# Attention and feed-forward on one core: another issue order and engine choice for the same 2621 pieces of work

## The chip, the cores and the metric

The kernel runs on one core of one Trainium2 chip. The metric is the device time of one execution in microseconds (us); lower is better. A core has TensorE (PE, its weight loads PEld), VectorE (DVE), ScalarE (ACT), GpSimd (POOL) and SyncE (SP), which here only issues transfers. Each engine takes its instructions strictly in the program's order.

## The reference

Rotary attention over 4 batches of 8 heads (576 positions, head size 64), then a feed-forward block with SiLU. Cut to what is computed:

```
q_rot, k_rot = (rotate(q), rotate(k))
scores = scale * np.matmul(q_rot, k_rot.transpose(0, 1, 3, 2))
scores = scores - np.max(scores, axis=-1, keepdims=True)
attn = np.exp(scores)
attn = attn / (np.sum(attn, axis=-1, keepdims=True) + 1e-09)
x = np.matmul(attn, v)            # then heads beside each other: 2304 x 512
h = x @ w_in                      # 512 x 2048
g = h * (1.0 / (1.0 + np.exp(-h)))
out = g @ w_out                   # 2048 x 512
```

## The kernel before

Heads go in pairs (4 pairs `p` a batch `b`). A batch's rows are split into two **units** of 256 rows (`u` = 0 to 7, the odd one with 64 more rows that are gathered in `x_rem` and make a ninth unit, `rem`). A **slot** is 128 rows of scores of one head (or 64 rows of both heads of a pair): 144 slots in all. The feed-forward's hidden size is cut in 8 steps of 256, so there are 9 x 8 = 72 steps.

f32 values go through the f16 matmul as a high part and a remainder. On every path that means two passes over a tile: `hi` (`part_hi`, L322: one scaled copy to f16, on ACT, DVE or POOL) and `lo` (`part_lo`, L328: the remainder, on DVE or POOL). **The engine decides how many instructions `lo` is:** on DVE it is one with two tensor inputs (L330); on POOL it is two, a scaling in place (L318) and a subtraction (L333):

```
if e is dve:
    dve.scalar_tensor_tensor(out=lo, in0=src, scalar=s, in1=hi, op0=ALU.mult, op1=ALU.subtract)
else:
    times(e, src, src, s, 1.0)
    e.tensor_tensor(out=lo, in0=src, in1=hi, op=ALU.subtract)
```

A slot (`add_slot`, L845) goes: `S` scores on PE (L865 for batch 0, where q and k are f32, L873 and L879 else) into one of two PSUM buffers `s`; `max` on DVE; `neg`; `exp` on ACT (L905) into `e` (3 buffers); `nr0`, `nr1` (sum and reciprocal); `hi` and `lo` into `pn` (3 buffers); `T`, a transposing transfer on SP's queue (L931, L934) into `pt`. The maximum has two forms. Engine letter `d`: a plain reduction (L894) that `neg` follows on ACT (L900) or DVE. Letter `D`: the scores are scaled in place, and the running minimum comes out with them (L889 and an accumulator read); no `neg` follows.

`add_pv` (L947) multiplies a pair's 4 or 5 transposed slots by v on PE (L972) and makes `xh` and `xl`. `add_step` (L1009) is one feed-forward step: `m1` (L1027, 24 matmuls), `tanh` on ACT (L1037, L1039), `g` on DVE (L1043), `gh` and `gl` as `hi` and `lo` above, and two `m2` (L1083). `add_qk` rotates q and k of batches 1 to 3 (`rope`, three passes, L534, L538, L541, on DVE or POOL), takes `qhi` and `qlo`, and transposes by transfer. `add_qk_first` does batch 0 in f32: PE transposes (`qP`), `qE` copies out of PSUM. `add_w` packs and splits the weights on their way in (`wld`, `wT`, `wC`, `wX`, `wtr`, `whi`, `wlo`). PE's stream mixes steps of unit `u` with the slots of later units.

**What sets the order.** Each of these pieces is a part with a number. `ORDER` (L38) is one list of all 2621 numbers, each with the letter of an engine: `t` PE, `a` ACT, `d` or `D` DVE, `p` POOL, `s` SP's queue, `A` a transfer on ACT's queue. The last loop of the kernel runs the parts in that order, and each engine gets its own parts in it. A part that waits holds up all parts behind it on its engine. Buffers rotate in the order of first use.

Of the kernel before, what the change touches and what calls it, by code (L numbers as in the profile page):

```python
# [43 lines left out]
509d 536s 718a 731d 74p 732a 556s 719d 733a 721t 89d 722d 723d 724a 711s 90t 739t 87d 702s 734d 720s 40d 91d 41d 735d
97s 70p 557a 736a 95s 740d 741d 742a 743a 522t 521d 725d 42d 43p 737d 523d 86s 537a 524t 525d 726d 727p 738s 538a 748t
96s 526t 92d 44s 744d 745a 75d 527d 749D 528d 750d 728d 729s 746p 751a 752a 71t 775t 93d 72a 106d 99a 45d 529d 540s
753d 98a 76t 776d 777a 778a 112d 539d 747s 77a 784t 757t 754a 558a 785d 94d 786a 532p 755d 779a 113p 758D 759d 559d
530a 114p 533p 787a 1981t 1982a 766t 760a 1983d 761d 762d 584s 793t 100t 534a 531d 780d 101d 781d 102d 763a 764p 542a
# [20 lines left out]
985a 2123t 2120d 991t 127d 1004a 986d 992d 971p 987d 988p 2124a 2125d 1009t 668a 167d 1005d 972s 2126p 1010D 993a
1999t 994a 149s 2000d 151a 989d 990s 995a 671p 1006a 1011a 2001d 1007d 996d 997p 2121t 2122t 1018t 152t 1012a 1036t  # L70
669d 2130t 1008s 672a 2127p 2128t 153d 154d 1013a 1037d 998d 1038a 999s 1039a 2129t 1019d 1020a 1040a 155d 126d 1014d
1015p 677d 2131a 2132d 1021a 2133a 190s 673d 1016d 1022a 179s 1023d 156a 1027t 1028d 2134p 1029a 1024a 1030a 1041d
# [1123 lines left out]
```

## Time and profile before

| | us |
|---|---|
| time, median of 3 runs | 687.45 (685.22 to 689.85) |
| the profiled execution, its own time | 688.31 |
| its span, first to last instruction | 686.5 |

PE is busy for 90% of the span, DVE for 73%, POOL for 61%, ACT for 57%. PE's granted clock is 0.93 over the span. The profile gives each engine's busy time by stretch, groups of equal instructions with their mean duration, and who ended an engine's idle time. A busy engine can also be an engine that waits inside an instruction, so for the instructions of interest the shortest duration stands beside the mean.

### The profile page before, as it was taken

How to read it: one execution, taken by the hardware profiler on the slowest of the kernel's cores; microseconds unless marked ns; L12 is line 12 of the kernel's file. 1: busy time of each engine (PE TensorE's matmuls, PEld its weight loads, DVE VectorE, ACT ScalarE, POOL GpSimd, SP SyncE). 2: the span in 40 equal slices, each digit the busy share in tenths (PEclk: the TensorE clock that was granted, in tenths of full speed). 3: DMA queues.
4: the chain of work that ended last, by engine and by line, in shares of the span. 5: the costliest groups of instructions: out<-in, count | busy, mean ns of one | idle time of the engine just before them, and what ended most of it. 6: DMA issues, size and time to landing. Idle time of an engine off the chain costs nothing. (4 is left out here: it accounts for less than half of the span.)

```text
span 686.5 us, 12772 instructions
## 1 busy us (share of the span) xinstructions
PE 618.2 (90%) x4524; PEld 403.1 (59%) x4524; DVE 500.1 (73%) x1095; ACT 390.1 (57%) x828; POOL 419.9 (61%) x375
## 2 busy tenths in 40 slices
PE   2788779989998999998999899899999899999996
PEld 1555546655655566665656566565666666666663
DVE  4776878999899789897898898788787476421222
ACT  1556776787677686675656565655645555212221
POOL 0564688879875556775767848776695675222321
PEclk9755657999999999999999999999999999999999
DMA  6898847978886958889795786987775575510201
GB/s 183 237 240 194 208 112 186 237 182 195 150 163 120 191 93 180 141 149 146 154 206 89 144 159 139 174 154 157 131 128 87 76 121 96 84 32 1 48 1 31
DMA packets 227888, 94.73 MB, mean 138 GB/s; under 512 B 206704, under 2 KB 211568, under 8 KB 227824
## 3 DMA queue, kind: packets, MB, share of 16 engines
q1 hardware_dynamic: 227344, 93.03, 66.6%
q10 hardware_dynamic: 480, 0.89, 0.9%
q8 instruction: 35, 0.57, 0.3%
q14 instruction: 29, 0.24, 0.1%
HBM read 35.55 MB, written 4.72 MB: 59 GB/s over the span
## 5 line engine op out<-in xcount | busy, mean ns | idle before, releaser
L1027 PEld LDWEIGHTS <-w_in 128*128 128x128 f16 x1728 | 168.5, 99 | 41.7 <-issue 7.7
L1027 PE MATMUL m<-xh,w_in 128*128 128x256 f16 x1024 | 182.9, 277 | 4.2 <-DVE g L1043 3.7
L1083 PE MATMUL m<-w_out,gh 128*128 128x512 f16 x576 | 173.3, 383 | 0.6 <-DVE ob L318 0.6
L905 ACT ACTIVATE e<-s,small 128x576 f32<-128x576 f32 x144 | 111.9, 777 | 73.5 <-DVE small L318 19.0
L1027 PE MATMUL m<-xl,w_in 128*128 128x256 f16 x512 | 141.7, 277 | 3.3 <-DVE xl L990 3.3
L1083 PE MATMUL m<-w_out,gl 128*128 128x512 f16 x288 | 110.2, 383 | 2.4 <-POOL gl L333 2.1
L1043 DVE SCALAR_TENSOR_TENSOR g<-g,m 128x512 f32<-128x512 f32 x72 | 49.0, 681 | 71.0 <-ACT g L1039 39.3
L333 POOL TENSOR_TENSOR pn<-e,pn 128x576 f16<-128x576 f32 x68 | 96.6, 1420 | 5.7
L318 POOL TENSOR_SCALAR e<-e,small 128x576 f32<-128x576 f32 x68 | 65.9, 969 | 49.7 <-ACT pn L324 28.3
L894 DVE TENSOR_REDUCE small<-s 128x1 f32<-128x576 f32 x97 | 72.2, 748 | 21.3 <-PE s L865 15.8
L330 DVE SCALAR_TENSOR_TENSOR pn<-e,small,pn 128x576 f16<-128x576 f32 x76 | 78.0, 1029 | 13.1 <-ACT pn L324 7.2
L1083 PEld LDWEIGHTS <-gh 128*128 128x128 f16 x576 | 53.2, 100 | 54.4 <-issue 4.5
L318 POOL TENSOR_SCALAR pn<-e,small 128x576 f16<-128x576 f32 x52 | 46.7, 899 | 54.4 <-DMA pt<-pn 23.2
L873 PE MATMUL s<-Tk,Tq 128*128 128x512 f16 (+1 forms) x384 | 62.1, 287 | 12.0 <-ACT e L905 10.6
L324 ACT ACTIVATE pn<-e,small 128x576 f16<-128x576 f32 x71 | 54.7, 770 | 30.2 <-DMA pt<-pn 15.0
L1039 ACT ACTIVATE g<-m,small 128x512 f32<-128x512 f32 x64 | 43.6, 681 | 49.0 <-PE m L1027 37.0
L972 PE MATMUL pv<-pt,vh 128*64 128x256 f16 (+1 forms) x576 | 64.9, 297 | 1.4 <-DVE small L299 0.9
L318 POOL TENSOR_SCALAR g<-g,small 128x512 f32<-128x512 f32 x37 | 28.9, 780 | 58.4 <-ACT gh L324 41.8
L865 PE MATMUL s<-Tk,Tq 64*128 64x512 f32 (+3 forms) x160 | 57.8, 561 | 3.3 <-ACT e L905 3.0
L873 PEld LDWEIGHTS <-Tq 128*128 128x128 f16 x384 | 29.6, 99 | 40.1 <-issue 16.2
L1083 PEld LDWEIGHTS <-gl 128*128 128x128 f16 x288 | 28.4, 98 | 39.8 <-POOL gl L333 5.0
L333 POOL TENSOR_TENSOR gl<-g,gh 128x512 f16<-128x512 f32 x37 | 48.1, 1301 | 3.1
(166 smaller groups left out, 998.6 us busy)
## 6 DMA issues: line engine op xcount, KB each, us to landing
w_out<-in_moe_w_out_dram SPq DMA_DIRECT2D x4, 1024.0 KB, 5.5
w_in<-in_moe_w_in_dram SPq DMA_DIRECT2D x4, 1024.0 KB, 6.0
out_dram<-ob SPq DMA_DIRECT2D x28, 128.0 KB, 2.4
io<-in_q_dram SPq DMA_DIRECT2D x12, 288.0 KB, 3.5
io<-in_k_dram SPq DMA_DIRECT2D x12, 288.0 KB, 3.8
io<-in_v_dram SPq DMA_DIRECT2D x12, 288.0 KB, 4.0
io<-in_v_dram SPq DMA_DIRECT2D x13, 256.0 KB, 4.4
ring<-in_moe_w_in_dram SPq DMA_DIRECT2D x3, 1024.0 KB, 6.8
```

Of the source, the lines that this page charges most:

```text
L318: e.tensor_scalar(out=out, in0=in0, scalar1=s1, scalar2=s2, op0=ALU.mult, op1=ALU.bypass if s2 is None else ALU.mult)
L324: act.activation(hi, src, AF.Copy, scale=s)
L330: dve.scalar_tensor_tensor(out=lo, in0=src, scalar=s, in1=hi, op0=ALU.mult, op1=ALU.subtract)
L333: e.tensor_tensor(out=lo, in0=src, in1=hi, op=ALU.subtract)
L865: pe.matmul(o[:, c0:c1], tq[hs, qs], tk[hs, c0:c1], start=True, stop=True)
L873: pe.matmul(o, tq[:, j, 2 * c:2 * c + 2, :], kt[:, r0:r1, js], start=(n == 0), stop=(n == 1))
L894: dve.reduce_max(out=m_of(0, 1), in_=buf("s", i)[:, 0:S], axis=AX.X)
L905: act.activation(buf("e", i), buf("s", i)[:, 0:S], AF.Exp, bias=m_of(1, 2), scale=-1.0 if fused[i] else cc[0], accum_out=m_of(2, 3),)
L972: pe.matmul(o[64 * j:64 * j + 64, 0:m], vt[part][:, j, s, :], pt[:, a, j, 0:m], start=(z == 0), stop=(z == len(steps) - 1),)
L1027: pe.matmul(t[:, c, 0:n], w[:, wz, kk, fs], xx[:, kk, 0:n], start=(kk == 0 and x == 0), stop=(kk == KD - 1 and x == 2),)
L1043: dve.scalar_tensor_tensor(out=g, in0=g, scalar=1.0, in1=t, op0=ALU.add, op1=ALU.mult)
L1083: pe.matmul(o, gs[gz][:, c, ts], w[:, wz, c], start=(first and c == 0 and x == 0), stop=(last and c == 1 and x == 2),)
```

## The change

Only `ORDER` changes. The same 2621 parts stand in another order, with other letters for 549 of them (476 if the two forms of `max` count as one); no instruction's shape changes. The list's first line:

```
-494s 4s 496p 495a 497d 0d 1s 10d 3s 5d 2s 11d 12d 25s 13t 6d 14a 7d 8t 490s 9a 31d 26d 15s 32d 27d 500t 501d 685t 491a
+494s 3s 496d 495a 1s 4s 497d 2s 5d 10d 6d 11d 12d 13t 14a 25s 26d 7d 490s 31d 27d 8t 32d 57s 9d 685t 28p 491a 492a
```

PE's own sequence keeps its shape: parts change places with near neighbours. The engines' letters, counted over both lists (parts that changed sides cancel):

| part | before | after |
|---|---|---|
| `lo` (remainder of a slot) | DVE 76, POOL 68 | DVE 89, POOL 55 |
| `gl` (remainder of a step) | DVE 35, POOL 37 | DVE 49, POOL 23 |
| `qlo` | DVE 16, POOL 8 | DVE 21, POOL 3 |
| `hi` (high part of a slot) | ACT 71, DVE 21, POOL 52 | ACT 88, DVE 22, POOL 34 |
| `rope`, single passes | DVE 51, POOL 45 | DVE 58, POOL 38 |
| `max`, form `d` / form `D` | 97 / 47 | 58 / 86 |
| `neg` that is left | ACT 61, DVE 36 | ACT 35, DVE 23 |
| `nr0` | ACT 79, DVE 65 | ACT 87, DVE 57 |
| `qE` | ACT 8 | ACT 4, DVE 4 |
| `vhi` | ACT 11, DVE 1, POOL 4 | ACT 10, DVE 5, POOL 1 |

Three places in the order. First DVE, just ahead of the last `xl` of unit 1 (L990), for which the first step of that unit waits. The names are tiles with the number of the buffer: `rt` and `io` belong to `rope`, `vl` to v's remainder, `pn` and `e` to a slot. Before:

```order
L534 TENSOR_TENSOR rt_1998<-io_1965,sin_t_124 128x576
L330 SCALAR_TENSOR_TENSOR pn_1986<-e_1961,small_118,pn_1986 128x576
L330 SCALAR_TENSOR_TENSOR vl1_130<-io_1689,small_118,vh_1850 128x320
L894 TENSOR_REDUCE small_118<-s_1993 128x1
L990 SCALAR_TENSOR_TENSOR xl_1401<-pv_2003,small_118,xh_1400 128x256
L990 SCALAR_TENSOR_TENSOR x_rem1_122<-pv_2003,small_118,x_rem0_121 128x64
```

After:

```order
L894 TENSOR_REDUCE small_118<-s_1944 128x1
L919 RECIPROCAL small_118<-small_118 128x1
L534 TENSOR_TENSOR rt_2009<-io_1912,sin_t_124 128x576
L330 SCALAR_TENSOR_TENSOR vl1_130<-io_1754,small_118,vh_1904 128x320 x2
L990 SCALAR_TENSOR_TENSOR xl_1343<-pv_1961,small_118,xh_1342 128x256
L990 SCALAR_TENSOR_TENSOR x_rem1_122<-pv_1961,small_118,x_rem0_121 128x64
L330 SCALAR_TENSOR_TENSOR pn_1949<-e_1937,small_118,pn_1949 128x576
```

The slot's remainder (`pn`) moved from ahead of `xl` to behind it; a second piece of v's remainder moved ahead of it.

Second POOL, over the slots 70, 68 and 71 ahead of the score matmul of slot 76 in unit 4. Before:

```order
L318 TENSOR_SCALAR g_3448<-g_3448,small_118 128x512
L333 TENSOR_TENSOR gl_3471<-g_3448,gh_3464 128x512
L318 TENSOR_SCALAR pn_3487<-e_3400,small_118 128x576
L318 TENSOR_SCALAR e_3400<-e_3400,small_118 128x576
L333 TENSOR_TENSOR pn_3487<-e_3400,pn_3487 128x576
L318 TENSOR_SCALAR pn_3597<-e_3467,small_118 128x576
L318 TENSOR_SCALAR vh_3537<-io_3444,small_118 128x1152
L318 TENSOR_SCALAR e_3516<-e_3516,small_118 128x576
L333 TENSOR_TENSOR pn_3611<-e_3516,pn_3611 128x576
```

After:

```order
L318 TENSOR_SCALAR e_3280<-e_3280,small_118 128x576
L333 TENSOR_TENSOR pn_3370<-e_3280,pn_3370 128x576
L318 TENSOR_SCALAR pn_3483<-e_3427,small_118 128x576
L318 TENSOR_SCALAR e_3427<-e_3427,small_118 128x576
L333 TENSOR_TENSOR pn_3483<-e_3427,pn_3483 128x576
L318 TENSOR_SCALAR e_3509<-e_3509,small_118 128x576
L333 TENSOR_TENSOR pn_3589<-e_3509,pn_3589 128x576
```

A step's remainder (`gl`), the high part of slot 68 (`pn_3597`) and v's high part (`vh`) are gone from POOL's list here; the latter two stand on ACT now.

Third SP's queue, where the first transposes of slots (L931) stand among the weights (L717, L723). Before:

```order
L717 DMA ring<-in_moe_w_in_dram 128x4x512
L628 DMA vh<-vh 64x2x256
L629 DMA vh<-vh 64x2x256
L723 DMA w_in<-in_moe_w_out_dram 128x1024
L931 DMA_TRANSPOSE pt<-pn 128x9x128
L717 DMA w_in<-in_moe_w_in_dram 128x4x512 x2
```

After:

```order
L717 DMA ring<-in_moe_w_in_dram 128x4x512
L717 DMA w_in<-in_moe_w_in_dram 128x4x512
L723 DMA w_in<-in_moe_w_out_dram 128x1024 x2
L931 DMA_TRANSPOSE pt<-pn 128x9x128 x2
L498 DMA io<-in_q_dram 128x576
```

One more load of each weight stands ahead of the first transpose, and the swap of v's halves (`vh`) went further back.

## Rows read from the trace of the kernel before

**Rows 1.** The page: busy time, share of the span, instructions.
```profile
PE 618.2 (90%) x4524; PEld 403.1 (59%) x4524; DVE 500.1 (73%) x1095; ACT 390.1 (57%) x828; POOL 419.9 (61%) x375
```

**Rows 2.** Windows: stretch, length, busy of PE, PEld, DVE, ACT, POOL; PE's clock; DMA.
```profile
17.00:117.00 100.00, 81.94 (x458) 54.36 (x455) 76.06 (x175) 65.08 (x121) 65.09 (x51) 0.61 0.76 196
117.00:171.00 54.00, 48.76 (x319) 30.84 (x316) 51.48 (x99) 42.37 (x80) 46.96 (x34) 0.97 0.90 207
171.00:540.00 369.00, 345.81 (x2711) 223.82 (x2712) 312.96 (x710) 232.71 (x520) 249.87 (x224) 0.98 0.79 144
600.00:686.50 86.50, 81.09 (x552) 53.61 (x550) 18.64 (x28) 20.04 (x48) 22.61 (x26) 0.99 0.10 22
```

**Rows 3.** Timeline at unit 1's first step: start, us, instruction [idle before, releaser].
```profile
203.25 1.83 DVE L330 SCALAR_TENSOR_TENSOR pn<-e,small,pn 128x576 f16<-128x576 f32 x1
...
205.00 1.68 DVE L330 SCALAR_TENSOR_TENSOR vl<-io,small,vh 128x320 f16<-128x320 f32 x1
...
207.79 0.37 PE L1027 MATMUL m<-xl,w_in 128*128 128x256 f16 x1 [2.95 <-DVE xl L990]
```

**Rows 4.** One line's instructions, L330 and L541: ns minimum/median/maximum, first and last start.
```profile
L330 DVE SCALAR_TENSOR_TENSOR pn<-e,small,pn x76: 796/819/2004, 44.6 to 587.3; 128x576 f16<-128x576 f32 x76
L330 DVE SCALAR_TENSOR_TENSOR gl<-g,small,gh x35: 725/752/1911, 132.6 to 678.2; 128x512 f16<-128x512 f32 x35
L330 DVE SCALAR_TENSOR_TENSOR vl<-io,small,vh x25: 540/701/1679, 51.7 to 518.3; 128x320 f16<-128x320 f32 x24, 128x640 f16<-128x640 f32 x1
L541 DVE TENSOR_TENSOR io<-io,rt x16: 741/756/1831, 84.7 to 475.9; 128x576 f32<-128x576 f32 x16
```

**Rows 5.** Timeline ahead of slot 76's scores.
```profile
322.72 0.74 POOL L318 TENSOR_SCALAR pn<-e,small 128x576 f16<-128x576 f32 x1 [3.96 <-DMA pt<-pn]
...
323.50 1.77 DVE L330 SCALAR_TENSOR_TENSOR pn<-e,small,pn 128x576 f16<-128x576 f32 x1 [3.43 <-POOL pn L318]
...
326.92 0.38 PE L873 MATMUL s<-Tk,Tq 128*128 128x512 f16 x1 [2.57 <-ACT e L905]
```

**Rows 6.** What SP's queue waited for: us in total, times, longest.
```profile
SPq L931 <- POOL pn L333: 35.7, 15, 6.4
SPq L931 <- POOL pn L318: 20.1, 10, 4.6
SPq L931 <- DVE pn L330: 17.2, 10, 2.4
```

**Rows 7.** Page, groups: line, engine, tiles, count | busy us, mean ns | idle before.
```profile
L318 POOL TENSOR_SCALAR e<-e,small 128x576 f32<-128x576 f32 x68 | 65.9, 969 | 49.7 <-ACT pn L324 28.3
L333 POOL TENSOR_TENSOR pn<-e,pn 128x576 f16<-128x576 f32 x68 | 96.6, 1420 | 5.7
L318 POOL TENSOR_SCALAR g<-g,small 128x512 f32<-128x512 f32 x37 | 28.9, 780 | 58.4 <-ACT gh L324 41.8
L333 POOL TENSOR_TENSOR gl<-g,gh 128x512 f16<-128x512 f32 x37 | 48.1, 1301 | 3.1
L318 POOL TENSOR_SCALAR pn<-e,small 128x576 f16<-128x576 f32 x52 | 46.7, 899 | 54.4 <-DMA pt<-pn 23.2
L330 DVE SCALAR_TENSOR_TENSOR pn<-e,small,pn 128x576 f16<-128x576 f32 x76 | 78.0, 1029 | 13.1 <-ACT pn L324 7.2
```

**Rows 8.** Groups by line and shape, whole span: `rope`, `hi`, forms of the maximum.
```profile
L538 POOL TENSOR_TENSOR io<-io,cos_t 128x576 f32<-128x576 f32 x16 | 25.7, 1607 | 9.9 <-ACT e L905 3.6 <-ACT small L900 2.4 <-issue 2.1
L324 ACT ACTIVATE pn<-e,small 128x576 f16<-128x576 f32 x71 | 54.7, 770 | 30.2 <-DMA pt<-pn 15.0 <-DVE small L919 9.6 <-DVE pn L330 2.0
L894 DVE TENSOR_REDUCE small<-s 128x1 f32<-128x576 f32 x97 | 72.2, 748 | 21.3 <-PE s L865 15.8 <-PE s L873 4.2 <-PE s L879 1.2
L889 DVE TENSOR_SCALAR_CACHE_REDUCE s<-s,small 128x576 f32<-128x576 f32 x42 | 34.2, 814 | 1.9 <-PE s L873 1.3 <-DVE small L318 0.5
L318 DVE TENSOR_SCALAR small<-small 128x1 f32<-128x1 f32 x67 | 12.4, 186 | 0.8
L889 DVE DVE_READ_ACCUMULATOR s<-s,small 128x1 f32 x42 | 5.9, 140 | 0.0
```

More of the change, by code (lines that the diff above doesn't have):

```diff
@@ L44 @@
[L44 to L48, printed above, removed]
@@ L69 @@
[L69 to L72, printed above, removed]
-1042d 1054t 199d 1025d 158d 1055d 2002t 2003a 2004d 2135t 192a 2136d 157d 1045t 1046d 1047d 2141t 191a 1043p 1017s
@@ new lines @@
+967a 968a 969d 667d 2117a 970p 2118d 979a 1000t 1001d 136d 982t 971d 1997a 1998d 1002a 1003a 980p 2123t 670a 972s
+2119a 983d 984d 178d 981s 671p 150s 668a 991t 992D 2115d 985a 986d 987d 127d 993d 994a 1004d 2120d 988a 672a 1009t
+2124a 989d 995d 1010d 1999t 1011a 2125d 1012a 990s 996d 997a 1013a 2126p 1036t 669d 1005d 1037d 1014d 2121t 2127d
+2130t 1006a 1038a 998d 1007d 2000a 1015a 1039a 677d 1018t 1019d 2122t 2128t 151a 2131a 1016p 2001d 190s 199d 192a 152t
+200p 1027t 2129t 673d 2132d 1028d 1020a 1021a 999s 153d 1040d 1022d 1023d 1054t 1024d 2133a 1029a 1008s 1030a 179s
@@ new lines @@
+1248d 1281d 1282a 1271D 1259d 1260s 2018a 2212d 1283a 2206t 1261t 1262d 1272d 299p 235d 2207t 1263d 1284d 1273a 1249p
+1250p 1306t 1274d 250s 292a 2216a 1275d 2213t 2217d 300d 1264a 2019d 1307d 2214t 1288t 1289D 2222t 1265a 1276a 1277d
+1251s 291a 293t 2218p 2219d 1285a 1286d 1290a 2220t 306d 1291a 1308a 2223a 2224d 1309a 251a 2140s 2225a 307d 1278s
+1315t 1292d 1310a 294d 295d 296d 1293d 1294a 297d 2226d 236d 301p 2229t 2221t 308p 266d 267d 249s 302a 303d 2230a
+2231d 252t 1311d 2227t 1295d 2232a 253d 309d 1297t 1298D 1266d 1299d 1312a 1313p 254d 255d 256a 1316D 2020t 1317a
@@ new lines @@
+2438t 1882t 1846t 1809s 1914d 1915p 2442a 2443d 2444p 2448t 1827s 1847D 1848a 1849a 2065t 1881s 1883D 1884d 1918t
+2445d 1916d 1917s 2449a 2450d 1885a 1861p 1864t 1862d 1886a 1850a 1851d 2451d 1852p 2066a 1853p 1919D 2439a 1865D
+2446t 2455t 2200s 1866a 1867a 1868a 1869d 2452d 1863s 1920d 1921a 1922a 1870d 2447t 2456a 1891t 2457d 1854s 2067d
+1892d 1871p 2458a 1872s 1954t 1893d 1894a 2459p 2462t 1955d 1923d 2453t 1924a 1925d 2463a 1887d 1888a 1889d 2454t
+2464d 2465a 2466p 1900t 1901d 1956d 1895a 1896d 1902d 1897d 1898d 1890s 1903a 1957a 2469t 1958d 1936t 1937D 1938a
@@ new lines @@
+1927t 2437s 1904a 1905d 2470a 1939a 2460t 1906p 1907p 2471d 1928D 1929a 1930a 2461t 2467t 1931a 2472a 1932d 1899s
+1945t 2473d 1908s 2468t 1933p 1934d 1935s 2476t 1972t 1959d 1960a 1940d 1946D 1941d 1947a 2477a 2478d 2068t 2483t
+1948a 1963t 1973D 1926s 1974d 1961p 1962s 2479a 2480d 1949a 1975a 1976d 1977d 1978p 2474t 2475t 2069a 2481t 2484a
+1950d 2070d 1951p 1979d 1980s 1952d 1953s 2485d 2490t 2380s 1942p 1964d 1943p 1965d 1966a 1967a 1968d 2071t 1969a
+1970p 1944s 2072d 2073d 2486a 2487p 2482t 2491a 1971s 2492d 2488t 2489t 2074t 2075d 2493p 2494p 2495t 2076d 2501t
@@ new lines @@
+2498t 2496a 2502a 2503d 2504d 2499d 2508t 2505d 2506t 2509a 2510d 2511d 2507t 2515t 2512p 2513t 2516a 2517d 2440s
+2518p 2514t 2519p 2522t 2523a 2524d 2520t 2521t 2529t 2525d 2526p 2530a 2531d 2527t 2532p 2528t 2533d 2536t 2537a
+2534t 2535t 2538d 2539d 2540d 2543t 2544a 2545d 2546p 2547d 2541t 2542t 2550t 2551a 2552d 2500s 2553d 2554d 2548t
+2549t 2561t 2555t 2558t 2562a 2563d 2564p 2565p 2568t 2559d 2560s 2566t 2556a 2569a 2570d 2567t 2575t 2571a 2572p
+2573t 2574t 2576a 2577d 2578d 2579p 2582t 2580t 2583a 2584d 2585a 2581t 2586d 2589t 2590a 2591d 2592d 2593p 2587t
@@ L165 @@
+2588t 2596t 2597a 2598d 2594t 2599p 2595t 2603t 2600p 2601t 2604a 2602t 2605d 2606p 2607d 2610t 2611a 2612d 2613d
+2614d 2497s 2608t 2557s 2609t 2615t 2618t 2616d 2619a 2617s 2620s
 """
```

213 lines of the change are left out of this document (98 added, 115 removed).

## The prediction

> **What bounds the kernel now.** The first view to read is the line of busy times [rows 1]. PE works for 618.2 of 686.5 us, so it is the engine that everything else serves. DVE (500.1) and POOL (419.9) are far from full over the whole span, so neither is a bound by its sum. The second view cuts the span into stretches [rows 2]. From 17 to 117 us the clock granted to PE is 0.61, between its two levels of 1.2 and 2.4 GHz, and PE idles 18 us of 100. From 600 us on, PE works 81.09 of 86.5 us at 0.99: nothing is to be had there. What an order can win lies mostly between 117 and 540 us. PE idles 54 − 48.76 = 5.24 us and 369 − 345.81 = 23.19 us there, and the missing clock costs 0.03 × 54 + 0.02 × 369 = 9.0 us. Together that is **37.4 us lost** in 423.
>
> The third view is the timeline at two of those losses. At 207.79 us PE starts the first step of unit 1 after 2.95 us of idling for `xl` [rows 3]. Ahead of `xl` on DVE stood a slot's `lo` of 1.83 us and v's `vl` of 1.68 us. The shortest of these instructions take 0.796 and 0.540 us [rows 4], so 1.03 + 1.14 = 2.2 us of the delay was not work: the instruction sat on DVE and waited inside. The same line shows a longest `lo` of 2.004 us beside that shortest, 1.2 us more. At 322.7 us [rows 5] the chain starts on POOL: it had waited 3.96 us for a `pn` buffer (which a transpose had to leave), then made a `hi`; DVE's `lo` came after 3.43 us of idling for that `hi`, again 1.77 us long; a little later PE had idled 2.57 us. So one stall is DVE late behind POOL's work, and one is POOL itself late.
>
> The fourth view says who is late with the slots' tiles: the transposes' queue waited 35.7 + 20.1 us for POOL's two passes over `pn`, and 17.2 us for DVE's [rows 6]. POOL has 55.8 of these 73.0 us, 76%.
>
> **The change part by part.** It moves work off POOL, and mostly onto DVE; no work for PE is added or removed.
>
> *What POOL loses.* A slot's `lo` on POOL is 0.969 + 1.420 = 2.389 us, a step's `gl` 0.780 + 1.301 = 2.081 us, a `hi` 0.899 us [rows 7], a `rope` pass 1.607 us [rows 8]. So 13 `lo` make 31.1 us, 14 `gl` 29.1, 18 `hi` 16.2, 7 passes of `rope` 11.2, and 5 `qlo`, of `lo`'s shape, 11.9. The sum is −99.5: POOL falls from 419.9 to about 320 us, by a quarter.
>
> *What DVE gets.* At the shortest durations [rows 4]: 13 `lo` × 0.796 = 10.3, 14 `gl` × 0.725 = 10.2, 5 `qlo` × 0.796 = 4.0, 7 `rope` × 0.741 = 5.2. The maximum in form `D` takes 0.814 us and an accumulator read of 0.140, where form `d` takes 0.748 [rows 8]: 39 × 0.206 = +8.0, against 13 `neg` × 0.186 = −2.4. Four `qE`, four `vhi` and one `hi` are nine more passes over a tile, 7.2 us at 0.796, against eight small `nr0`, −1.5 at 0.186; I count +5. The sum is **+40**. How long the added passes sit waiting isn't shown. The mean `lo` is 1.029 us [rows 7], 0.233 over the shortest, so 39 added passes (13 + 14 + 5 + 7) would add 9.1 us if POOL were as busy as now. With a quarter less on POOL the 76 `lo` alone save 76 × 0.233 / 4 = 4.4. I take 0, between −4 and +9. DVE then has 540 us.
>
> A rule of the Trainium skill bears on this ("SBUF — State Buffer", section "SBUF: two separate sides"). It says that DVE and GpSimd share a pair of ports as an exclusive lock: a DVE instruction with two SBUF inputs and a GpSimd one keep each other out for a whole instruction. The trace agrees in size: 2.004 − 0.796 = 1.2 us fits in one POOL pass of 1.3 to 1.42 us. By the rule, the work that has to share the pair falls by POOL's 100 us and grows by DVE's 30 us of two-input passes, 70 us less in all; by the rows alone I leave the waiting as it is.
>
> *What ACT gets.* 17 `hi` × 0.770 = 13.1 us [rows 8] less 26 `neg`, which by DVE's price of 0.186 are −4.8: about +8 on 390, where it is 57% busy. It hides beside PE's work. Without that cover it would cost at most those 8 us.
>
> *Where it lands.* The losses of 117 to 540 us are mostly waits for a tile that POOL or DVE made too late. POOL's 76% of the transposes' waits shrink when its queue goes from 70% full ((46.96 + 249.87) / 423) to about 53%; I take half of them away: 0.76 × 0.5 = 0.38. Not all losses are such waits, so I take a third of 37.4: **−12.5 us**. The ends are nothing, if POOL's waits are only replaced by others, and 0.6 of the losses, −22.
>
> DVE pays. From 117 to 171 us it is busy for 51.48 of 54 us. Its share of the +40 by busy time is 40 × 51.48 / 500.1 = 4.1 us, which makes 55.6 for 54 us. DVE has no idle left to hide that, and here it stretches PE's path by some 2 to 4 us: **+3**. From 171 to 540 us it gets 40 × 312.96 / 500.1 = 25 us, 338 of 369, and I let its 56 us of idle time hide that.
>
> *Moves that I cost at nothing.* SP's queue has one more load of each weight ahead of the first transpose. The first steps need the weights anyway, and PE's work from 17 to 117 us idles 18 us for several causes that stay; if the transposes came late by a load, it is 2 us at most by the longest waits for DVE's `pn` [rows 6]. ACT gets the `hi` of slot 68 and v's `vh` just where POOL had waited 3.96 us [rows 5]: that gain is part of the third above. At unit 1's first step the `lo` goes behind `xl`, but a second `vl` comes ahead of it: 0.796 out, 0.540 in at the shortest, so that stall stays near 2.7 us [rows 3, 4]. The stretch from 600 us on is not touched.
>
> *The sum.* 686.5 − 12.5 + 3 = 677.0 us of span. The profiled execution's own time is 688.3 for this span, 1.8 more, and the median of the runs shown is 0.9 below that execution. So 677.0 + 1.8 − 0.9 = **678 us**, 1.4% below the median.
>
> **The rivals.** *It is seen nowhere.* PE's idle is made of waits for the next link of a slot's chain, and when POOL gets out of the way another link takes its place. For it: POOL itself idles 54.4 us ahead of its `hi`, mostly for transposes, and 49.7 ahead of its `lo`, mostly for ACT [rows 7]. An engine that waits so much is not what limits the stream; the buffers are. Against it: the stall of [rows 5] goes through POOL. If two thirds of the 12.5 are given back, and DVE's 3 stay, it is 687.45 − 4.2 + 3 = 686 us.
>
> *DVE becomes the bound (slower).* Place: 117 to 540 us. DVE's 364.4 us of work there become 394 of 423, 93%, and its idle time falls from 58.6 to 29 us. DVE waits 21.3 us for PE's scores ahead of the `max` [rows 8], which no order fully removes, because only two score buffers stand. It decides when more than about 30 us of DVE's idle cannot be filled: from there each microsecond that DVE gets is one for PE. A third of the added 29 us on the path, with no gain from POOL, gives 687.45 + 9.7 = 697 us. For it: 51.48 of 54 us are DVE's already, and unit 1 waits for DVE [rows 3]. Against it: the waiting inside DVE's passes should shrink with POOL's work. If instead all 39 added passes met a POOL pass at the 1.2 us of the longest one, it would be 47 us more on DVE, and far above 700.
>
> **How the numbers follow.** I give the forecast 0.42, the unseen change 0.36 and the bound DVE 0.22. One per cent, 7 us, is about what a measurement of this kernel can tell from no change. The forecast's own range follows from its third: with 0.6 of the losses won and DVE's +3 it is 668; with a fifth won (−7.5) and +3 it is 683. Those above 680.6 count as the same, but there are few, and some of the second case falls below it: faster 0.42, same 0.36, slower 0.22. The range for 8 in 10 starts at 665 (the low end with DVE's waiting 4 us shorter) and goes to 698, just over the slower rival's time.
>
> **What would show it.** In the profile after, POOL should be busy for about 320 us and DVE for about 540; a DVE sum under 530 means that its passes wait less inside, with a mean `lo` under 1.0 us. PE's idle and lost clock from 117 to 540 us should sum to about 25 us instead of 37.4, and the wait for slot 76's scores should be gone or short. The transposes should wait much less than 55.8 us for POOL. From 117 to 171 us I expect DVE to be full and PE not better. The prediction is wrong at its third if POOL is 100 us lighter and PE's losses are unchanged, and wrong at its +3 if DVE's idle time vanishes beyond 171 us as well and PE waits for DVE's `pn` and `xl` more than before. It would be wrong outside its steps if the stretch up to 117 us, which I leave alone, moved by more than 3 us: there the clock is 0.61, so anything that starts PE's steady work earlier or later is worth more than it looks.

## The result and the profile after

The changed kernel takes **651.0 us** (median of 4 runs, 649.1 to 654.1) against 686.8 for the kernel before on the same chip. The ratio is 0.948 with a 95% interval of 0.943 to 0.953: 36 us faster, where 9 were forecast and the range ended at 665. The profiled execution has a span of 650.0 us.

The line of busy times, which answers [rows 1]:

```profile
PE 611.8 (94%) x4524; PEld 403.0 (62%) x4524; DVE 488.6 (75%) x1153; ACT 397.8 (61%) x832; POOL 307.5 (47%) x280
```

POOL lost 112 us, ACT gained 8, and DVE lost 11.5 although 58 more of its instructions stand there. The windows, with the columns of [rows 2] (stretch, length, busy time and count of PE, PEld, DVE, ACT, POOL, PE's clock, DMA share, GB/s). The third ends where PE stands at the same work as at 540 us before, to within a step; the last begins 36 us earlier for the same reason:

```profile
17.00:117.00 100.00, 88.25 (x490) 59.87 (x491) 82.91 (x201) 67.67 (x123) 49.03 (x38) 0.90 0.81 202
117.00:171.00 54.00, 49.75 (x314) 31.52 (x313) 47.16 (x104) 41.62 (x82) 27.32 (x23) 0.94 0.94 214
171.00:508.00 337.00, 334.56 (x2702) 219.50 (x2701) 297.56 (x732) 243.13 (x527) 185.05 (x165) 0.99 0.87 156
564.00:650.00 86.00, 81.09 (x552) 53.70 (x551) 22.23 (x34) 16.78 (x43) 18.97 (x22) 1.00 0.08 19
```

From 171 us on PE idles 2.4 us in 337, where it idled 23.2 in 369. The gain has an exact place. Unit 1's first step starts at 203.6 us before and at 203.0 after, so nothing is won until then. Unit 6's first step starts at 534.3 and at 502.9, which is 30.8 us of the 36 in between; the other 5 come behind it, where PE stops idling too. One window of each kernel between these two steps, before and after:

```profile
203.60:534.30 330.70, 307.89 (x2443) 200.43 (x2442) 280.25 (x626) 207.91 (x463) 222.76 (x198) 0.98 0.77 143
```

```profile
203.00:502.90 299.90, 298.74 (x2451) 197.76 (x2450) 266.74 (x648) 214.95 (x468) 167.97 (x149) 1.00 0.89 160
```

PE idles 22.8 us of the first and 1.2 of the second; its clock goes from 0.98 to 1.00, and its busy time falls by 9.2 us. The two sum to the 30.8. PE has nothing left to lose there. Part of the busy time was the clock's: right behind the stalls of [rows 3] and [rows 5], which lasted 2.95 and 2.57 us, PE works without a pause at 0.50, the lower of its two levels. Two windows of the kernel before:

```profile
207.80:210.80 3.00, 3.00 (x15) 2.14 (x15) 2.85 (x5) 0.83 (x2) 1.54 (x2) 0.50 0.00 0
328.00:330.00 2.00, 2.00 (x12) 1.40 (x10) 1.52 (x3) 0.90 (x4) 2.00 (x2) 0.50 1.05 183
```

So each of these stalls cost more than its idle time, and between the two steps the changed kernel has no such stretch.

Which waits of PE went shows in the groups by line and shape. First the kernel before, the row with the scores of batches 1 to 3, then the same row after, where the slots' other groups stand with it (busy us, mean ns | idle before and releasers):

```profile
L873 PE MATMUL s<-Tk,Tq 128*128 128x512 f16 x192 | 59.4, 381 | 12.0 <-ACT e L905 10.6 <-DMA Tq<-n 1.0
```

```profile
L873 PE MATMUL s<-Tk,Tq 128*128 128x512 f16 x192 | 58.3, 380 | 0.4 <-ACT e L905 0.2
L324 ACT ACTIVATE pn<-e,small 128x576 f16<-128x576 f32 x88 | 67.2, 768 | 11.8 <-DVE small L919 4.5 <-ACT e L905 2.9 <-DMA pt<-pn 2.0
L889 DVE TENSOR_SCALAR_CACHE_REDUCE s<-s,small 128x576 f32<-128x576 f32 x62 | 50.3, 817 | 6.7 <-PE s L873 4.5 <-PE s L879 1.2 <-ACT pn L324 0.7
```

From 117 us on PE's largest wait in total was for `exp`, which frees a score buffer: 10.6 us, now 0.2. For a transposed tile (`pt`) none of PE's matmuls waited in the old trace, and its weight loads only 1.1 us. How POOL reaches `exp` shows in the kernel before at the stall of [rows 5], on ACT:

```profile
325.38 0.78 ACT L324 ACTIVATE pn<-e,small 128x576 f16<-128x576 f32 x1 [4.11 <-DVE small L919]
326.06 0.72 ACT L905 ACTIVATE e<-s,small 128x576 f32<-128x576 f32 x1
```

POOL's `hi` was late for want of a `pn` buffer; DVE's `lo` waited for it; the reciprocal (L919) stood behind that `lo` on DVE; ACT's next `hi` waited 4.11 us for the reciprocal; and the `exp` that PE wanted stood behind that `hi` on ACT. The first link is what got lighter: the idle time ahead of `hi` for a `pn` buffer fell from 23.2 us on POOL and 15.0 on ACT [rows 7, 8] to 2.9 and 2.0. The slots' remainders, answering [rows 7] and [rows 4]: first groups of the page, then one line's shortest, median and longest durations in ns.

```profile
L318 POOL TENSOR_SCALAR e<-e,small 128x576 f32<-128x576 f32 x55 | 48.1, 875 | 95.3 <-ACT pn L324 74.4
L330 DVE SCALAR_TENSOR_TENSOR pn<-e,small,pn 128x576 f16<-128x576 f32 x89 | 77.7, 878 | 5.9 <-ACT pn L324 3.4
L333 POOL TENSOR_TENSOR pn<-e,pn 128x576 f16<-128x576 f32 x55 | 74.6, 1356 | 4.6
```

```profile
L330 DVE SCALAR_TENSOR_TENSOR pn<-e,small,pn x89: 797/812/1715, 33.9 to 544.6; 128x576 f16<-128x576 f32 x89
L330 DVE SCALAR_TENSOR_TENSOR gl<-g,small,gh x49: 726/746/1250, 119.1 to 642.1; 128x512 f16<-128x512 f32 x49
L330 DVE SCALAR_TENSOR_TENSOR vl<-io,small,vh x25: 527/548/1562, 45.3 to 494.1; 128x320 f16<-128x320 f32 x24, 128x640 f16<-128x640 f32 x1
```

DVE makes 89 remainders in 77.7 us, where 76 took 78.0 [rows 7]: the mean fell from 1029 to 878 ns, since fewer of them wait inside. What they wait for is POOL: before, 31 of the 76 took more than 860 ns, and every one of these ended 0.60 to 0.62 us after the end of a POOL pass; after, it is 16 of 89, with the same 0.60 to 0.62 us. What the transposes' queue waited for, answering [rows 6]:

```profile
SPq L931 <- DVE pn L330: 29.4, 13, 7.1
SPq L931 <- POOL pn L333: 15.3, 11, 3.0
SPq L931 <- POOL pn L318: 15.0, 8, 3.2
```

For POOL 30.3 us instead of 55.8, for DVE 29.4 instead of 17.2. Last the two places of the timeline. Unit 1's first step, answering [rows 3]:

```profile
201.91 1.01 DVE L330 SCALAR_TENSOR_TENSOR vl<-io,small,vh 128x320 f16<-128x320 f32 x2
202.83 0.48 DVE L990 SCALAR_TENSOR_TENSOR xl<-pv,small,xh 128x256 f16<-128x256 f32 x1
...
203.42 0.81 DVE L330 SCALAR_TENSOR_TENSOR pn<-e,small,pn 128x576 f16<-128x576 f32 x1
```

And around slot 76's scores (312.73 us), answering [rows 5]:

```profile
302.34 0.75 POOL L318 TENSOR_SCALAR pn<-e,small 128x576 f16<-128x576 f32 x1 [4.15 <-DVE small L919]
...
305.23 0.78 ACT L324 ACTIVATE pn<-e,small 128x576 f16<-128x576 f32 x1 [0.71 <-DMA pt<-pn]
...
312.73 0.65 PE L873 MATMUL s<-Tk,Tq 128*128 128x512 f16 x4
```

At the first place two `vl` take 1.01 us together instead of one taking 1.68, and no idle time of PE is left. At the second, slot 68's `hi` is on ACT, which waits 0.71 us for the `pn` buffer where POOL had waited 3.96; POOL still idles 4.15 us a little earlier, and it costs nothing: PE goes into slot 76 without a wait.

### The profile page after: what moved, and what is told of

It reads as the page before. It is cut to its first block, busy times and chain, and to the rows that moved or that the text cites. A ratio compares the mean times of both kernels' runs of the same rounds, so it can differ in the third digit from the quotient of the medians.

```text
span 650.0 us, 12729 instructions
## 1 busy us (share of the span) xinstructions
PE 611.8 (94%) x4524; PEld 403.0 (62%) x4524; DVE 488.6 (75%) x1153; ACT 397.8 (61%) x832; POOL 307.5 (47%) x280
## 4 chain that ended last, share of the span: by engine, by line
PE 52%; POOL 6%; DVE 6%; issue 4%; DMA 3%; ACT 2%; SPq 0%; POOLq 0%; DVEq 0%; ACTq 0%
PE m L1027 20%; PE m L1083 20%; PE pv L972 5%; PE s L873 4%; DMA pt<-pn 2%; POOL pn L333 2%; DVE pn L330 1%; POOL e L318 1%; PE s L865 1%; DMA io<-in_v_dram 1%; ACT e L905 1%; DVE s L889 1%; ACT pn L324 1%; PE s L879 1%; DVE small L894 1%
## 5 line engine op out<-in xcount | busy, mean ns | idle before, releaser
L1027 PE MATMUL m<-xh,w_in 128*128 128x256 f16 x1024 | 178.4, 273 | 1.5 <-DVE g L1043 1.2
L1043 DVE SCALAR_TENSOR_TENSOR g<-g,m 128x512 f32<-128x512 f32 x72 | 49.0, 681 | 63.4 <-ACT g L1039 33.6
L318 POOL TENSOR_SCALAR e<-e,small 128x576 f32<-128x576 f32 x55 | 48.1, 875 | 95.3 <-ACT pn L324 74.4
L330 DVE SCALAR_TENSOR_TENSOR pn<-e,small,pn 128x576 f16<-128x576 f32 x89 | 77.7, 878 | 5.9 <-ACT pn L324 3.4
L333 POOL TENSOR_TENSOR pn<-e,pn 128x576 f16<-128x576 f32 x55 | 74.6, 1356 | 4.6
L324 ACT ACTIVATE pn<-e,small 128x576 f16<-128x576 f32 x88 | 67.2, 768 | 11.8 <-DVE small L919 4.5
L865 PE MATMUL s<-Tk,Tq 64*128 64x64 f32 (+3 forms) x160 | 59.9, 566 | 4.0 <-ACT e L905 2.1
L318 POOL TENSOR_SCALAR pn<-e,small 128x576 f16<-128x576 f32 x34 | 32.1, 944 | 52.5 <-DVE small L919 28.4
L889 DVE TENSOR_SCALAR_CACHE_REDUCE s<-s,small 128x576 f32<-128x576 f32 x62 | 50.3, 817 | 6.7 <-PE s L873 4.5
L865 PEld LDWEIGHTS s<-Tk,Tq 64*128 64x128 f32 (+1 forms) x160 | 30.0, 232 | 34.4 <-issue 27.8
L1083 PEld LDWEIGHTS <-gl 128*128 128x128 f16 x288 | 28.4, 99 | 35.2 <-issue 1.1
L894 DVE TENSOR_REDUCE small<-s 128x1 f32<-128x576 f32 x58 | 43.5, 749 | 8.9 <-PE s L865 6.7
L972 PEld LDWEIGHTS <-vh 128*64 128x64 f16 x576 | 36.0, 116 | 14.4 <-issue 7.8
```

The source lines that it names most:

```text
L318: e.tensor_scalar(out=out, in0=in0, scalar1=s1, scalar2=s2, op0=ALU.mult, op1=ALU.bypass if s2 is None else ALU.mult)
L324: act.activation(hi, src, AF.Copy, scale=s)
L865: pe.matmul(o[:, c0:c1], tq[hs, qs], tk[hs, c0:c1], start=True, stop=True)
L889: dve.tensor_scalar(out=t, in0=t, scalar1=cc[1], scalar2=None, op0=ALU.mult, op1=ALU.min, accum_out=m_of(1, 2),)
L894: dve.reduce_max(out=m_of(0, 1), in_=buf("s", i)[:, 0:S], axis=AX.X)
L972: pe.matmul(o[64 * j:64 * j + 64, 0:m], vt[part][:, j, s, :], pt[:, a, j, 0:m], start=(z == 0), stop=(z == len(steps) - 1),)
```

## The experiments

Every kernel was timed in several rounds beside the kernel before on the same chip; these had medians of 684.4 to 686.4. Two changed kernels are compared by their ratios to it; the intervals of such a difference are 4 to 6 us either way. Four theories: **L**, POOL's load is what PE waited for; **O**, the sequence is the gain; **M**, sequence and engines fit each other; and DVE as the bound.

### One half of the change alone: letters or sequence

The letters of after in the sequence of before (here two of the 549 places):

```diff
-... 2162t 1077d 1078p 1108t 1085a 1086d 1087a 1071s 211s ...
+... 2162t 1077d 1078a 1108t 1085d 1086d 1087a 1071s 211s ...
```

> Every part stands where the kernel before has it and gets the engine letter of the changed kernel (549 letters differ). Theory L (load): PE's waits were waits behind POOL, so 112 us less on POOL, and the shorter DVE passes that come with it, are the gain: about 655 us, with PE idle under 8 us from 203 us on. Theory O (order): the gain is in the sequence, so this stays at 680 to 690. Theory M (match): letters and sequence were chosen for each other, and either alone is no better than before, 685 or more.

The letters of before in the sequence of after:

```diff
-... 214t 1092a 1099t 188d 1085d 189d 215d 1093a 1094d ...
+... 214t 1092d 1099t 188d 1085a 189d 215d 1093a 1094a ...
```

> The changed kernel's sequence with every part on the engine that the kernel before gives it. Theory L: POOL is as full as before (about 420 us) and the losses stay, 680 to 690. Theory O: about 655. Theory M: 685 or more.

Letters alone (e1): **739.8 us**, ratio 1.081 (1.079 to 1.084). Sequence alone (e2): **756.9 us**, 1.106 (1.100 to 1.111). Each half costs 55 to 72 us, and both together win 36. The windows between the same two steps (unit 1's first, unit 6's first), letters alone and then sequence alone:

```profile
218.80:580.60 361.80, 313.09 (x2442) 201.79 (x2441) 276.46 (x648) 213.56 (x467) 165.75 (x148) 0.98 0.71 130
```

```profile
232.90:599.00 366.10, 315.83 (x2452) 202.74 (x2451) 271.59 (x628) 209.59 (x463) 216.93 (x200) 0.98 0.70 131
```

Compare the first with the changed kernel's window. DVE, ACT and POOL do the same work within 4% (276 against 267, 214 against 215, 166 against 168 us), and PE idles 48.7 us instead of 1.2. Busy times therefore do not tell the time of this kernel: with equal loads the stretch lasts 361.8 or 299.9 us. Theories L and O fall as single causes, and M stands, though both halves are far worse than its "no better than before". With the letters alone, PE's wait for `exp` grows instead of going (the row of the scores of batches 1 to 3, three lines further down in this file):

```profile
L876 PE MATMUL s<-Tk,Tq 128*128 128x512 f16 x192 | 61.0, 388 | 18.8 <-ACT e L908 18.5
```

### One half of the program alone

Before's list up to unit 1's first step, then after's list for all parts that are left, and the reverse:

```diff
 ... 192a 2136d 157d 1045t 1046d 1047d
-2141t 191a 1043p 1017s 193t 194d 1056a 195d ...
+200p 1031a 1017s 1032d 1056a 205d 2141t 1026s ...
```

> Sequence and letters of the kernel before up to unit 1's first step (the first 812 parts, 203 us), all the rest in sequence and letters of the changed kernel. The traces of before and after reach that step at 203.6 and 203.0 us, so if the gain is made where it shows, this gives 651 to 656. Rival: the changed kernel brings a lead into that point (weights and tiles that are ready ahead), and without it half of the 36 us is lost, about 668.

```diff
 ... 2135t 205d 2003a 158d 157d 2004d
-2141t 1042a 180s 1025d 1026s 1043d 1044s 191a ...
+180s 1042d 1025d 2136d 1045t 1046d 1047d 2141t ...
```

> The other half: the changed kernel's sequence and letters up to unit 1's first step, then those of the kernel before. If the gain is made where it shows: 684 to 690. Rival (a lead that is brought along): about 668.

The late half alone (e3) gives **657.1 us**, 0.961 (0.958 to 0.963); the early half (e4) **680.0**, 0.994 (0.992 to 0.996). So 27 us are made from unit 1 on, where the traces show them, and 4 with the early half; some 5 us, little more than the interval, are there only with both. Both results lie just outside what was expected without a lead (651 to 656, 684 to 690). The early half may carry a small one along: its one trace is 1.2 us ahead of the kernel before at unit 1's first step (202.4 us) and 7.2 at unit 6's (527.1).

### POOL's load without moving anything

In before, sequence and letters untouched, POOL's remainders are made lighter (they are left out: zeros):

```diff
-            times(e, src, src, s, 1.0)
-            e.tensor_tensor(out=lo, in0=src, in1=hi, op=ALU.subtract)
+            part = src[..., 0:16]
+            times(e, part, part, s, 1.0)
+            e.tensor_tensor(out=lo, in0=hi, in1=hi, op=ALU.subtract)
```

> The kernel before, sequence and letters untouched, with POOL made lighter on the spot: in a remainder on POOL the scaling pass runs over 16 columns instead of all, and the subtraction takes the high part twice, so that the remainders made on POOL are left out (zeros). POOL should lose 80 to 120 us, as much as by the change. Theory L (POOL's load is what PE waits for): 650 to 665. Theory M (each sequence holds its own waits, load matters little): 680 or more. The prediction's own size for this relief, without DVE's added work, is 675.

This is e5: **670.6 us**, 0.978 (0.971 to 0.984). POOL is busy for 341.8 us, 78 less, so the relief on the spot is worth 15 us (11 to 20), 0.19 us for each us of POOL. It lies between the two expected ranges:

```profile
PE 609.7 (92%) x4524; PEld 401.2 (61%) x4524; DVE 475.5 (72%) x1095; ACT 388.8 (59%) x828; POOL 341.8 (52%) x375
```

DVE's busy time falls by 24.6 us with it [rows 1], although nothing was moved to or from DVE: this much of its waiting inside hung on POOL in the traced run (664.5 us, the fastest of the four). The edit is not quite load alone, since the lighter subtraction no longer reads `e`, whose buffer can come free earlier.

The opposite in after: POOL gets load back, which nobody waits for, behind 39 remainders of slots and 21 of steps that stand on POOL (in `flo` and `fgl`, with `u != 0` for the steps):

```diff
+            if e == "p" and i >= 40:
+                wide = sin_t[:, 0:7].rearrange("p a b c -> p (a b c)")
+                eng[e].tensor_tensor(out=ring[:, 2, 0:448], in0=wide, in1=wide, op=ALU.subtract)
```

> The changed kernel, sequence and letters untouched, with POOL loaded again from unit 1's first step on: behind each remainder on POOL (40 of slots, 21 of steps) a further two-input pass of 128x448 on constants, whose result nobody uses. That adds about 61 x 1.1 = 67 us to POOL there, which is what the letters had taken from it in that stretch. Theory L: most of the 36 us comes back, 675 to 690. Theory M: 651 to 658.

This is e6: **668.7 us**, 0.976 (0.972 to 0.979): by the ratios 19 us (15 to 23) more than the changed kernel, for 66 us of added passes, 0.29 us a us. Neither L nor M as I had put them: about half of the gain goes with the load. Its twin adds work to POOL that reads nothing:

```diff
+            if e == "p" and i >= 40:
+                eng[e].memset(ring[:, 2], 0.0)
```

> The twin of e6: at the same 60 places POOL fills a tile of 128x1024 with zeros instead of the two-input pass, so POOL gets work that reads nothing (meant to be about as long as the 1.1 us of e6's pass; its length shows in the trace). If POOL's load hurts because DVE's two-input passes wait inside for it, DVE's mean slot remainder stays near the 0.88 us of the changed kernel and the time at 651 to 656. If it hurts because POOL itself comes late, the time rises as in e6, to 663 to 670, in proportion to the added time.

This is e9: **662.3 us**, 0.966 (0.962 to 0.971): 13 us (8 to 17) more for 57 us of fills, 0.22 us a us. The rows of e6, then of e9 (the window between the two steps, PE's scores of batches 1 to 3, the added work where it is one group, DVE's remainder):

```profile
204.30:519.50 315.20, 302.27 (x2452) 198.17 (x2451) 284.65 (x650) 215.59 (x470) 213.32 (x189) 1.00 0.82 152
...
L873 PE MATMUL s<-Tk,Tq 128*128 128x512 f16 x192 | 58.9, 380 | 9.6 <-ACT e L905 9.4
...
L330 DVE SCALAR_TENSOR_TENSOR pn<-e,small,pn 128x576 f16<-128x576 f32 x89 | 84.3, 952 | 6.6 <-ACT pn L324 3.1
```

```profile
202.80:512.50 309.70, 301.32 (x2452) 197.93 (x2451) 276.91 (x649) 214.50 (x468) 201.01 (x189) 1.00 0.84 155
...
L873 PE MATMUL s<-Tk,Tq 128*128 128x512 f16 x192 | 58.8, 380 | 6.8 <-ACT e L905 6.5
...
L927 POOL MEMSET ring<- 128x1024 f32 x39 | 37.1, 950 | 0.0
...
L330 DVE SCALAR_TENSOR_TENSOR pn<-e,small,pn 128x576 f16<-128x576 f32 x89 | 80.6, 910 | 6.7 <-ACT pn L324 3.3
```

With either load PE's wait for `exp` comes back, 9.4 and 6.5 us instead of 0.2: a part that nobody waits for holds up the parts behind it. With the two-input pass DVE's mean remainder rises from 878 to 952 ns, with the fill to 910, and DVE's busy time rises from 488.6 to 510.1 and 498.6 us. Much of the price is there with the fill, which disturbs DVE less. This suggests that POOL's load hurts by making POOL's own tiles late as well as through DVE's waiting inside its passes; how much falls to each is not shown. The intervals of the two rates overlap (0.14 to 0.30 and 0.23 to 0.35), and DVE waited more with the fill too.

### Is DVE the bound?

A small pass behind 108 remainders on DVE in after:

```diff
+            if e in "dD" and i >= 40:
+                times(dve, ring[:, 2, 0:1], sin_t[:, 0, 0, 0:1], 1.0, 1.0)
```

> The changed kernel with a small pass of 128x1 (about 0.19 us) behind each of some 100 remainders on DVE from unit 1's first step on: about 20 us more for DVE, which is as much as e6 added to DVE by waiting. If DVE bounds the stretch: 665 to 672. If the tiles come early enough that PE does not notice: 651 to 656.

This is e11: **652.5 us**, 0.951 (0.946 to 0.956): 2 us more, between 3 less and 7 more, not to be told from the changed kernel. The added work and the window:

```profile
L318 DVE TENSOR_SCALAR ring<-sin_t 128x1 f32<-128x1 f32 x108 | 15.6, 144 | 0.0
...
206.10:508.20 302.10, 299.46 (x2452) 197.99 (x2451) 272.02 (x736) 214.97 (x469) 167.24 (x149) 1.00 0.88 159
```

DVE has 15.6 us more to do (144 ns each, not the 190 that I had reckoned with), at 90% busy, and PE idles 2.6 us. DVE is not the bound: one us for each us would have been 15.6. A price as small as POOL's, 0.2 to 0.3 us a us, would lie within the interval. DVE's busy time over the whole span rose by 8.6 us only (497.2).

### Moving remainders in the old sequence

Before, with only those 59 remainders on DVE that the change takes from POOL:

```diff
-... 1088d 2164d 2161t 1109D 1097p 1110d 222d 223t 224d ...
+... 1088d 2164d 2161t 1109D 1097d 1110d 222d 223t 224d ...
```

> The kernel before in its own sequence, with only those 59 remainders (35 of slots, 24 of steps) on DVE that the change moves there from POOL; nothing goes the other way. POOL -134 us, DVE +45. Theory L: 660 to 675. DVE as the bound: 700 or more. Theory M: 690 to 720, since DVE's queue then holds passes at places that were planned for POOL.

This is e7: **692.1 us**, 1.010 (1.006 to 1.014). POOL is down to 283.1 us, 137 less, and the kernel is 7 us slower; e5, with 78 us less and nothing moved, won 15. The relief of e5 is more than lost here. PE's wait for POOL's `gl` falls from 2.1 to 0.9 us and that for `xl` from 3.3 to 0.5, but those for DVE's `g` (L1043 in before) and for `exp` grow, from 3.7 to 9.7 and from 10.6 to 13.0. The 59 passes now sit in DVE's queue at places that suited POOL's, ahead of what PE waits for.

### The forms of the maximum

Before, with after's forms (73 places), and after with before's:

```diff
-... 2006d 1098s 2007d 243d 1127d 1139d 1140d 231t 232d ...
+... 2006d 1098s 2007d 243d 1127D 1139d 1140d 231t 232d ...
```

> The kernel before in its own sequence, with only the forms of the maximum of the changed kernel (73 parts, 56 from d to D, 17 from D to d). Form D saves a slot's chain the neg with its hand-over (0.84 us of waiting and 0.25 of work on average in the stretch from 204 to 540 us) and costs DVE 8 us in all. If the shorter chain is the gain: 670 to 678. If not: 683 to 692.

```diff
-... 1139d 1140d 1158d 1141a 1127D 239p 1128a 2172a 1129a ...
+... 1139d 1140d 1158d 1141a 1127d 239p 1128a 2172a 1129a ...
```

> The changed kernel with the forms of the maximum of the kernel before (56 back from D to d, each with its neg, 17 the other way). If the forms are worth the same in either sequence: 651 + 8.6 = 660. If the sequence is matched to them: 670 or more. If form D only helps where PE waits anyway: 651 to 655.

In before they win 7.7 us (e8, **676.9**, 0.989, 0.984 to 0.993); in after they are worth 7, between 2 and 12 (e10, **655.3**, 0.958, 0.953 to 0.964). So they are worth about the same in both sequences, as far as the runs can tell. Form `D` saves a slot's chain the `neg` and its hand-over, and this alone, in the old sequence, is faster. With e5's lighter POOL on top (the remainders made on POOL are left out again; the edit is that of e5 and of e8 together):

> The kernel before, in its own sequence, with e5's lighter POOL and e8's forms of the maximum together (the remainders made on POOL are left out again). If the two gains add: 685.5 - 15 - 8.6 = 662. If both relieve the same waits: 668 or more. Where it stays above the changed kernel's 651, the rest is the sequence with the other letters.

This is e12: **668.1 us**, 0.974 (0.968 to 0.980), against 670.6 and 0.978 (0.971 to 0.984) for e5 alone: on top of e5 the forms win 3 us, give or take 6. Alone they won 7.7, which this interval takes in, so whether the two gains add or relieve the same waits stays open.

### What the sequence fits

Single families of letters, against what stands around them. After with before's engines for the high parts, then for the remainders; before with after's engines for the high parts:

```diff
-... 1100d 223t 224d 225d 1078a 1079p 228s 1108t 210s ...
+... 1100d 223t 224d 225d 1078p 1079p 228s 1108t 210s ...
```

> The changed kernel with the engines of the kernel before for the high parts of the slots alone (80 parts change engine, 18 more of them on POOL: about +16 us for POOL). By load at e6's rate (0.27 us a us of POOL): 651 + 4 = 655. If the sequence is matched to the engines, each part on another engine costs, whatever it does to POOL's load: 670 or more.

```diff
-... 1101a 2005t 1102a 1086d 1097d 1153t 1154d 1103d 2169t ...
+... 1101a 2005t 1102a 1086d 1097p 1153t 1154d 1103d 2169t ...
```

> The changed kernel with the engines of the kernel before for the remainders of slots and steps alone (91 parts change engine, 27 more of them on POOL: about +60 us for POOL). By load at e6's rate: 651 + 16 = 667. By matching: 690 or more.

```diff
-... 2163a 210s 1100d 221t 1096a 1079p 2160t 188d 1088d ...
+... 2163a 210s 1100d 221t 1096p 1079p 2160t 188d 1088d ...
```

> The kernel before in its own sequence, with the changed kernel's engines for the high parts of the slots alone (80 parts, 18 fewer on POOL, 17 more on ACT). By load: 685.5 - 4 = 681. By matching: 700 or more, part of the 55 us that all letters together cost in this sequence.

In this order e13, e14 and e16: **683.4** (0.996, 0.994 to 0.999), **701.3** (1.025, 1.022 to 1.028) and **710.1 us** (1.039, 1.036 to 1.043). The windows between the two steps, of the first and the last of them:

```profile
214.50:530.20 315.70, 302.38 (x2451) 198.89 (x2450) 271.49 (x651) 207.54 (x457) 180.59 (x163) 1.00 0.81 151
```

```profile
213.50:553.30 339.80, 309.50 (x2441) 200.62 (x2440) 268.38 (x624) 215.57 (x475) 210.56 (x185) 0.97 0.76 139
```

In the first, 80 high parts on other engines cost 33 us by the ratios. In its trace 16 of them lie in this stretch, where POOL has 13 us more, and 11.5 ahead of it; over the whole span POOL has 21 us more (328.3), which by e6's rate is worth 6. The remainders cost 53 us for 55 more on POOL (362.4), which is worth 16 by that rate. In the last, POOL and DVE have 12 us less each than in the kernel before, and the stretch takes 339.8 us instead of 330.7. PE's wait for `exp` in the row of the scores is 5.3, 19.4 and 17.9 us in the three. The cost comes with the changed engines, whichever way the load goes. The likely reason, as at the stall above: a part that takes another time, on another queue, holds up what stands behind it, and the order of what stands behind it was made for the other case.

### A mixture

Before with after's forms of the maximum up to unit 1's first step (e8 reached it at 198.6 us), then after:

> Up to unit 1's first step the kernel before with the changed kernel's forms of the maximum (which reached that step at 198.6 us in e8, 4.4 us ahead of the changed kernel), from there on the changed kernel. If the stretches are independent, as e3 and e4 suggest: 651 - 4.4 = 647, or 657 - 5 = 652 by e3.

This is e15: **654.0 us**, 0.955 (0.951 to 0.960); it does not beat the changed kernel. The 4.4 us of lead were not there to begin with: this trace reaches unit 1's first step at 203.9 us, and not at 198.6, after the same 812 parts. Traces of one and the same list differ by some us at this step (202.4 to 206.1 in five traces with the changed kernel's list up to there), so one trace of e8 was too little for a lead of 4.4.

## Why the prediction was wrong

**The direction was right, and so were the loads of POOL and ACT.** POOL was to fall to 320 us and fell to 307.5; ACT was to gain 8 and gained 7.7. POOL's sum had left out three `vhi`, and what stayed on POOL became shorter (the subtraction from 1420 to 1356 ns).

**The step that failed is "a third" of the 37.4 us.** It went from waits to time in one factor: POOL has 76% of the transposes' waits, half of them go, so 0.38 of PE's losses go. The waits nearly halved, from 55.8 to 30.3 us. But from 117 us to 540 (508 after) PE's idle time fell from 28.4 to 6.7 us (4.25 + 2.44), and with the missing clock (0.06 × 54 + 0.01 × 337 = 6.6) the losses fell from 37.4 to 13.3 us, where 25 were forecast. That is 24 us and not 12.5. The size was wrong because the wait was the wrong one: PE's matmuls waited for no transposed tile. They waited for `exp`, which stands behind late parts on ACT and DVE, and this wait went almost whole, from 10.6 to 0.2 us. A wait of a queue costs PE only what is left when PE wants the tile. With a sequence in which nearly every tile comes in time, queues still wait (29.4 us for DVE's `pn`, more than before; POOL idle 95.3 us ahead of its remainders) and PE doesn't. The top end of that term, 0.6 of the losses, was too low as well; "no loss is left" should have been an end of the range.

**DVE's waiting was mis-sized, its work was not.** The +40 and a waiting of 0 "between −4 and +9" should have made 540 us; it was 488.6. Counted over all groups of DVE at the shortest duration of each in either trace, the work went from 474 to 509 us, so the +40 was close. What the instructions take above that went from 91 to 53 us, 38 less. (These are sums of the single durations, which overlap a little and so add up to more than the busy time.) Of the slots' remainders alone: over the shortest 0.796 us, 89 have 89 × (0.878 − 0.796) = 7.3 us, where 76 had 17.7. And the +3 from 117 to 171 us was not there: DVE is busy for 47.16 of 54 us, not for 55.6. Above all, DVE's load was priced as time. e11 gives DVE 15.6 us more, and the time rises by 2 us, within its interval.

**The rule on the shared ports.** The Trainium skill ("SBUF — State Buffer", section "SBUF: two separate sides") was set beside the rows as an alternative to leaving the waiting unchanged. For a DVE instruction with two SBUF inputs the page limits the lock to a GpSimd operation that reads SBUF, which the prediction left out. The traces agree with the rule: with POOL 112 us lighter, the mean remainder went from 1029 to 878 ns, e6 took it back to 952, and every remainder over 860 ns, before and after, ends 0.60 to 0.62 us after a POOL pass. The forecast went by the rows alone and not by the rule. The rows alone gave me no reason to expect more than a quarter less for the 76; it was 10.4 us less of 17.7 in spite of 13 more passes.

**A term was missing.** Form `D` was costed as 5.6 us more work for DVE and nothing else. It takes the `neg` out of each slot's chain, and PE's largest wait from 117 us on in the old trace was for the end of this chain's first half (`exp`, 10.6 us). It was worth 7.7 us in the old sequence and about 7 in the new.

**The sequence was costed at nothing.** The prediction priced what moves between engines and looked at the order in three places only. e1 and e2 show that the fit between order and engines is worth more than everything in the sum: 55 and 72 us lost with either half. At the one stall where it looked at the order, unit 1's, it also misread the row: the first step started at 203.6 us and stood still in its middle until 207.79. The 2.7 us that it left there are gone. This could not be read from the loads, and three places were no sample for 2621 parts.

**The rivals.** "Seen nowhere" named the right mechanism, the next link taking the place of the last one, and e7 and e16 show it at work in the old sequence, where the waits for `exp` and `g` grow; the new sequence hardly has it. "DVE becomes the bound" is refuted by e11. The warning on the stretch up to 117 us came to little: PE's clock there is 0.90 instead of 0.61, unit 0's first step starts 3.3 us earlier (113.1 against 116.4), just beyond the 3 named but no more than traces of one list differ there, and of this 0.6 is left at unit 1's.

**What makes up the 36 us.** The load of POOL at 0.19 to 0.29 us a us (e5, e6) would be 21 to 32 us for its 112, an estimate by rates that were measured with nothing else moved; the forms of the maximum give 7 to 8. That leaves little or nothing for the order alone, whose part is that it lets the engines change without the 55 us that this costs in the old one. How the sum divides further stays open, since e12 does not tell whether the parts add. Which places of the new order make it fit the new engines is not shown either; e3 and e4 only show that most of them lie behind unit 1's first step.

## What to carry to other kernels

In a kernel whose engines run fixed queues, an engine choice and an order are one thing: cost an edit that changes both as a whole, with a range that reaches down to "PE never waits" and up to "the old order with the new engines". The idle time of the engine that bounds is the stake; the waits of the other engines and their busy shares say little about how much of it goes. A load that is taken away on the spot, and one that is put back with no consumer, are cheap ways to price an engine's lateness.

## What the runs showed of the hardware

PE's granted clock over the span did not go with the time: the four timed runs of the changed kernel had 0.973, 0.990, 0.946 and 0.945 and took 651.8, 654.1, 650.2 and 649.1 us. Nor does it settle the first stretch: e4, e6, e9 and e11 run the changed kernel's list unchanged up to unit 1's first step. From 17 to 117 us the five traces had clocks of 0.90 (changed kernel), 0.69, 0.68, 0.90 and 0.61, and reached unit 0's first step at 113.1, 111.9, 114.8, 113.1 and 116.9 us.

What a POOL pass does to DVE depends on both instructions. A fill, which reads no tile, took 950 ns for 128x1024 f32. In e9 a remainder (two tensor inputs) that ran beside a fill alone took its shortest time, 0.80 us, but a high part (one input, 0.51 us at the shortest) waited for the end of the fill and ended 0.31 us after it. Two places of e9:

```profile
477.86 0.94 POOL L1060 MEMSET ring<- 128x1024 f32 x1
...
478.19 0.80 DVE L330 SCALAR_TENSOR_TENSOR pn<-e,small,pn 128x576 f16<-128x576 f32 x1
```

```profile
329.46 0.95 POOL L927 MEMSET ring<- 128x1024 f32 x1
329.61 1.12 DVE L318 TENSOR_SCALAR pn<-e,small 128x576 f16<-128x576 f32 x1
```

The mean high part on DVE rose from 659 ns in the changed kernel to 927 in e9. The mean remainder rose from 878 to 910 there because 20 of the 89 instead of 16 took more than 860 ns, and each of these ended 0.60 to 0.62 us after a POOL pass that reads tiles.
